# Batch 0 of a fused attention and MLP kernel: single score products between other work, products on zeros, and other places for the weight transfers

## The chip, the cores and the metric

One core of a Trainium2 chip. The metric is the device time of one execution in microseconds. The profiled span of an execution is some 1.8 us shorter than its device time. In the views PE is TensorE (PEld its weight loads), ACT ScalarE, DVE VectorE, POOL GpSimd and SP the sync engine; PEclk is the share of its full clock that TensorE was granted.

## The reference

```python
def _attn_ref(q, k, v):                      # each 8 x 12 x 448 x 64 (batch, heads, sequence, head_dim)
    scores = (1.0 / np.sqrt(64)) * np.matmul(q, k.transpose(0, 1, 3, 2))
    attn = np.exp(scores - np.max(scores, axis=-1, keepdims=True))
    attn = attn / (np.sum(attn, axis=-1, keepdims=True) + 1e-09)
    return np.matmul(attn, v)

def _moe_ref(x, w_in, w_out):                # x 3584 x 768, w_in 768 x 2048, w_out 2048 x 768
    h = x @ w_in
    return np.maximum(0.01 * h, h) @ w_out
```

The attention output, heads side by side, is `x`.

## The kernel before

Work goes by head pairs: 6 pairs in each of 8 batches, so 48 units `u`. A pair's q, k and v are loaded in float32 (three loads of 0.229 MB), cast to bf16 on POOL (pair 0's q and k on DVE and ACT), and q and k are transposed. Then come four score products with an exponential each (one for each key chunk), and the product with v (PV). The MLP of a batch is a generator whose matmuls are spread over the attention steps of the next batch, so batch 0's attention has no MLP to run beside it.

```python
def load(u, queues=(nc.sync,) * 3): ...          # q, k, v of pair u; five buffers each
def cast(u, by=(nc.gpsimd.tensor_copy,) * 3): ...# to bf16 on POOL; v into v_sb
def load_w(n=1):                                 # the next n of 8 weight pieces: 4 of w_in, 4 of w_out
    for _ in range(n):
        if w_steps:
            o, i = w_steps.pop(0)
            nc.gpsimd.dma_start(out=o, in_=i)    # float32 in memory, bf16 on the chip: 0.786 MB written
...
NPE = 12
def dma_transposes(u):                           # q and k of pairs 12 and on
    if NPE <= u < NU:
        turn(qkT[u % NQ][:, :QL], ...)           # a DMA transpose from the sync queue
def transposes(u):                               # q and k of the pairs before 12
    if u >= min(NPE, NU):
        return
    tr = ps_tr.tile([P, 2, S], BF16, name="tr")
    for i in range(2):                           # q, then k
        for so in range(NSC):
            nc.tensor.transpose(tr[:, i, ts(so, SC)], qk_sb[u][:, i, so], ident[:SC, :SC])
    nc.vector.tensor_copy(qkT[u % NQ][:, :QL], tr.rearrange("p i s -> p (i s)"))
...
# one unit of work, steps s0 to s7 (guards left out)
s0: scores(u, 0); scores(u, 1); expo(u, 0)
s1: expo(u, 1); x_transposes(u - 2); dma_transposes(u + 2)
s2: pv(u - 1, 0)
s3: load(u + 5); load_w({2: 1, 3: 2, 4: 2, 5: 2}.get(u, 0)); transposes(u + 1)
s4: scores(u, 2); scores(u, 3); expo(u, 2)
s5: expo(u, 3); cast(u + 3)
s6: pv(u - 1, 1)
```

Scores have two buffers in PSUM. One weight piece is issued ahead of all this, after pair 0's casts. Eight products on zeros stand at the very start (1.19 to 4.56 us), meant for TensorE's clock; the granted clock is 1.00 from 4.20 to 7.61 us and 0.50 from there to 14.44.

The softmax here doesn't subtract the row's maximum and nothing guards it: scores larger than these inputs give would overflow.

## Time and profile before

| | before |
|---|---|
| time, median of the first 3 runs | 427.61 us (427.56 to 428.5) |
| profiled span | 425.7 us |
| TensorE busy | 411.4 us, 97% |
| TensorE busy in the first 36 us | 28.05 us |
| TensorE busy from 36 to 75 us | 38.49 of 39.00 us |
| transfer rate from 8 to 64 us | 245 to 263 GB/s |

TensorE is full from 36 us to the tail, so what the kernel can gain or lose lies before.

### The profile page before, as it was taken

What the parts mean: (1) busy time and instruction counts of PE and PEld (TensorE: products, weight loads), DVE (VectorE), ACT (ScalarE), POOL (GpSimd) and SP (SyncE); (2) the same over time, 40 slices, a digit from 0 to 9 for tenths busy, and PEclk for the clock granted to TensorE, in tenths of its full rate; (3) what the DMA queues carried; (4) which work ended last, traced back from release to release, by engine and by line L of the source; (5) the groups of instructions that cost most, each with busy time, mean ns of one, the idle gap of its engine ahead of it and who ended that gap; (6) DMA issues with size and microseconds to landing.
All of it is one profiled execution on the core that took longest, in us unless ns stands there. A gap on an engine that the chain in (4) does not pass through costs nothing.

```text
span 425.7 us, 8968 instructions
## 1 busy us (share of the span) xinstructions
PE 411.4 (97%) x3709; PEld 226.3 (53%) x3724; DVE 100.2 (24%) x271; ACT 229.9 (54%) x322; POOL 92.1 (22%) x168
## 2 busy tenths in 40 slices
PE   6889999999999999999999999999999999999995
PEld 2555655544555555544455555554455555654562
DVE  1454323211222212311123212321123211320021
ACT  4887774467534675466643576456743477214300
POOL 5583332422111313112211131221112100000000
PEclk8899999999999999999999999999999999999999
DMA  8999999995546765784464977667446450230022
GB/s 219 257 246 245 249 249 197 256 253 118 125 117 167 209 125 158 187 209 108 104 148 131 183 180 145 177 178 170 117 99 161 99 84 18 56 85 2 0 75 74
DMA packets 98505, 63.66 MB, mean 150 GB/s; under 512 B 55456, under 2 KB 94880, under 8 KB 98464
## 3 DMA queue, kind: packets, MB, share of 16 engines
q1 hardware_dynamic: 90928, 56.56, 55.3%
q0 software_dynamic: 7296, 6.29, 9.4%
q8 instruction: 29, 0.48, 0.5%
q10 hardware_dynamic: 240, 0.23, 0.2%
q14 instruction: 12, 0.10, 0.1%
HBM read 45.61 MB, written 11.01 MB: 133 GB/s over the span
## 4 chain that ended last, share of the span: by engine, by line
PE 83%; DMA 12%; POOL 2%; ACT 1%; issue 1%; DVE 0%; SPq 0%; POOLq 0%
PE mm L256 33%; PE mm L239 31%; PE pv L196 9%; PE sc L178 9%; DMA fv<-in_v_dram 5%; DMA qkT<-qkb 4%; DMA fk<-in_k_dram 2%; DMA xT<-x 1%; ACT e L187 1%; PE tr L166 1%; POOL w_out_sb L124 1%; POOL v L111 1%; POOL w_in_sb L124 0%; POOL qkb L109 0%; POOL qkb L110 0%
## 5 line engine op out<-in xcount | busy, mean ns | idle before, releaser
L187 ACT ACTIVATE e<-sc 112x896 bf16<-112x896 f32 x192 | 167.6, 915 | 107.2 <-PE sc L178 107.2
L239 PE MATMUL mm<-xT,w_in_sb 128*128 128x384 bf16 (+1 forms) x753 | 160.3, 352 | 0.8
L256 PE MATMUL mm<-w_out_sb,h 128*128 128x384 bf16 x896 | 160.2, 326 | 0.0
L256 PEld LDWEIGHTS <-h 128*128 128x128 bf16 x896 | 81.7, 98 | 62.4 <-issue 14.1
L239 PEld LDWEIGHTS <-w_in_sb 128*128 128x128 bf16 x768 | 68.3, 97 | 70.3 <-issue 16.3
L244 ACT ACTIVATE h<-mm 128x384 bf16<-128x384 f32 (+1 forms) x128 | 69.8, 545 | 60.0 <-PE mm L239 59.9
L111 POOL CAST v<-fv 112x512 bf16<-112x512 f32 x48 | 29.6, 617 | 196.1 <-PE pv L196 163.2
L196 PEld LDWEIGHTS <-e 112*128 112x128 bf16 x1536 | 61.4, 98 | 15.6 <-DVE x L204 1.9
L203 DVE RECIPROCAL rec<-pv 112x4 f32<-112x4 f32 x96 | 17.5, 183 | 206.1 <-PE pv L196 205.3
L196 PE MATMUL pv<-v,e 112*128 112x65 bf16 x1536 | 65.3, 194 | 0.1
L178 PE MATMUL sc<-qkT 64*128 64x448 bf16 x384 | 55.4, 360 | 6.0 <-ACT e L187 3.7
L261 DVE COPY o<-mm 128x384 f32<-128x384 f32 x56 | 31.2, 557 | 90.0 <-PE mm L256 89.9
L204 DVE TENSOR_TENSOR x<-pv,rec 112x256 bf16<-112x256 f32 x96 | 40.7, 424 | 3.5 <-DVE rec L203 0.3
L109 POOL CAST qkb<-fq 112x512 bf16<-112x512 f32 x47 | 28.9, 615 | 37.4 <-DMA fq<-in_q_dram 20.6
L178 PEld LDWEIGHTS <-qkT 64*128 64x128 bf16 x384 | 12.1, 94 | 37.7 <-issue 31.3
L110 POOL CAST qkb<-fk 112x512 bf16<-112x512 f32 x47 | 28.9, 614 | 11.8 <-DMA fk<-in_k_dram 11.6
L166 PE MATMUL tr<-ident,qkb 112*128 112x112 bf16 x96 | 7.8, 226 | 1.3 <-POOL qkb L109 0.8
L169 DVE COPY qkT<-tr 128x896 bf16<-128x896 bf16 x12 | 7.4, 620 | 5.4 <-PE tr L166 5.3
L166 PEld LDWEIGHTS <-qkb 112*128 112x128 bf16 x96 | 6.2, 104 | 3.6 <-POOL qkb L109 1.3
L218 DVE COPY xT<-tr 128x448 bf16<-128x448 bf16 x9 | 3.5, 392 | 12.1 <-PE tr L217 12.1
L134 PE MATMUL mm<-warm 128*128 128x512 bf16 x8 | 3.4, 600 | 1.2 <-DVE warm L131 1.2
L124 POOL DMA_DIRECT2D w_out_sb<-in_moe_w_out_dram x4 | 3.5, 877 | 0.0
(17 smaller groups left out, 14.1 us busy)
## 6 DMA issues: line engine op xcount, KB each, us to landing
fq<-in_q_dram SPq DMA_DIRECT2D x48, 224.0 KB, 3.9
fv<-in_v_dram SPq DMA_DIRECT2D x48, 224.0 KB, 4.3
fk<-in_k_dram SPq DMA_DIRECT2D x47, 224.0 KB, 4.1
w_in_sb<-in_moe_w_in_dram POOLq DMA_DIRECT2D x4, 768.0 KB, 15.1
w_out_sb<-in_moe_w_out_dram POOLq DMA_DIRECT2D x4, 768.0 KB, 35.3
out_dram<-o SPq DMA_DIRECT2D x8, 336.0 KB, 3.1
out_dram<-o SPq DMA_DIRECT2D x8, 288.0 KB, 2.7
out_dram<-o SPq DMA_DIRECT2D x8, 240.0 KB, 3.3
```

Of the source, the lines that this page charges most:

```text
L109: by[0](qk_sb[u][:, 0].rearrange("p so h d -> p h so d"), fq)
L110: by[1](qk_sb[u][:, 1].rearrange("p so h d -> p h so d"), fk)
L111: by[2](v_sb[u % NV][:, :, :, :D], fv)
L166: nc.tensor.transpose(tr[:, i, ts(so, SC)], qk_sb[u][:, i, so], ident[:SC, :SC])
L178: nc.tensor.matmul(ps[:, j, :S], t[j * D:(j + 1) * D, S + c * SC:S + c * SC + P], t[j * D:(j + 1) * D, :S], start=True, stop=True,)
L187: nc.scalar.activation(e[:, :, c, :], sc_t.pop((u, c))[:SC, :, :S], AX.Exp, scale=scale)
L196: nc.tensor.matmul(ps[:, qc, :], e[:, at:at + P], vt[:, j, c, :], start=(c == 0), stop=(c == NSC - 1),)
L204: nc.vector.tensor_mul(x_t[u][:, :, j, :], ps[:SC, :, :D], rec.to_broadcast([SC, NSC, D]))
L239: nc.tensor.matmul(ps[:, :n], w_in_sb[:, kk, ts(m, P)], xT[:, kk, at:at + n], start=(kk == 0), stop=(kk == KD - 1),)
L244: nc.scalar.activation(h[:, m, :n], ps[:, :n], AX.Prelu, alpha=0.01)
L256: nc.tensor.matmul(ps[:, :NW], h[:, m, ts(c, P)], w_out_sb[:, m, ts(w, NW)], start=(m == 0), stop=(m == MD - 1),)
L261: nc.vector.tensor_copy(o[c][:, ts(w, NW)], ps[:, :NW])
```

## The change

Its intent: in batch 0, where ACT's exponentials set the pace (four take 3.34 of a pair's 3.88 us), issue each score product as soon as its buffer is free, with other products between, so that ACT never waits. More products on zeros through the first chunks (called fillers below) are meant to hold TensorE's clock up. The weight pieces come one for each pair while they are pieces of w_in. A new `first_slots` serves `u` = 0 to 5.

```diff
-    for _ in range(8):
-        ps = ps_mm.tile([P, 512], F32, name="mm")
-        nc.tensor.matmul(ps, warm[:, :P], warm, start=True, stop=True)
+    def warm_up(n): ...                     # n such products
+    warm_up(9)
...
+    def first_slots(u):
+        s0: scores(u, 0); expo(u, 0); if u == 0: warm_up(2)
+        s1: x_transposes(u - 2)
+        s2: scores(u, 1); expo(u, 1); if u == 0: warm_up(2)
+        s3: load(u + 5); load_w({1: 1, 2: 1, 3: 1, 4: 2, 5: 2}.get(u, 0)); pv(u - 1, 0)
+        s4: scores(u, 2); expo(u, 2)
+        s5: cast(u + 3); transposes(u + 1)
+        s6: scores(u, 3); expo(u, 3)
+        s7: pv(u - 1, 1)
...
-            load_w({2: 1, 3: 2, 4: 2, 5: 2}.get(u, 0))
...
-    steps = [s for u in range(NU + 2) for s in slots(u)]
+    steps = [s for u in range(NU + 2) for s in (first_slots if u < HP else slots)(u)]
...
     transposes(0)
+    warm_up(2)
```

(The steps of `first_slots` are written in one line each here, without their guards.)

More of the change, by code (lines that the diff above doesn't have):

```diff
@@ L131, with warm_up @@
     nc.vector.memset(warm, 0.0)
-    for _ in range(8):
-        ps = ps_mm.tile([P, 512], F32, name="mm")
-        nc.tensor.matmul(ps, warm[:, :P], warm, start=True, stop=True)
+    def warm_up(n):
+        for _ in range(n):
+            ps = ps_mm.tile([P, 512], F32, name="mm")
+            nc.tensor.matmul(ps, warm[:, :P], warm, start=True, stop=True)
+    warm_up(9)
     ident = const_pool.tile([P, P], BF16)
@@ L264, in mlp, with s0, s1, s2 @@
                 yield NW
+    def first_slots(u):
+        def s0():
+            scores(u, 0)
+            expo(u, 0)
+            if u == 0:
+                warm_up(2)
+        def s1():
+            if u >= 2:
+                x_transposes(u - 2)
+        def s2():
+            scores(u, 1)
+            expo(u, 1)
+            if u == 0:
+                warm_up(2)
+        def s3():
+            load(u + 5)
+            load_w({1: 1, 2: 1, 3: 1, 4: 2, 5: 2}.get(u, 0))
+            if u >= 1:
+                pv(u - 1, 0)
+        def s4():
+            scores(u, 2)
+            expo(u, 2)
+        def s5():
+            cast(u + 3)
+            transposes(u + 1)
+        def s6():
+            scores(u, 3)
+            expo(u, 3)
+        def s7():
+            if u >= 1:
+                pv(u - 1, 1)
+        return [s0, s1, s2, s3, s4, s5, s6, s7]
     def slots(u):
@@ L318 @@
     transposes(0)
+    warm_up(2)
     for s in steps[:begin[0]]:
```

## The prediction

> **What bounds the kernel now.** I read the page's engine rows first, then its slices, the chain of waits, the timeline of the first 75 us, and the DMA queues in two stretches.
>
> ```profile
> PE   6889999999999999999999999999999999999995
> PEld 2555655544555555544455555554455555654562
> DVE  1454323211222212311123212321123211320021
> ACT  4887774467534675466643576456743477214300
> POOL 5583332422111313112211131221112100000000
> PEclk8899999999999999999999999999999999999999
> DMA  8999999995546765784464977667446450230022
> ```
>
> A slice is 10.6 us. PE is busy 97% of the span: after about 36 us TensorE never rests (25.00 of 25.00 us between 36.2 and 61.2). The only room is in the first three and a half slices and in the tail, which the change leaves alone. But the DMA row reads 9 from the second slice to the ninth: until some 85 us the transfers are as full as TensorE will be later. The timeline (start, duration, engine, instruction, idle time before it) shows batch 0:
>
> ```profile
> 28.38 0.56 PEld L166 LDWEIGHTS <-qkb 112*128 112x128 bf16 x8
> ...
> 29.29 0.63 POOL L110 CAST qkb<-fk 112x512 bf16<-112x512 f32 x1
> 29.50 3.34 ACT L187 ACTIVATE e<-sc 112x896 bf16<-112x896 f32 x4 [0.54 <-PE sc L178]
> ```
>
> Four exponentials take 3.34 us and ACT then idles 0.54 us because two score products stand together behind the transposes: 3.88 us for each head pair. This idle is what the change aims at. What feeds TensorE's transposes is the cast of q and k on POOL:
>
> ```profile
> 32.42 0.56 PE L166 MATMUL tr<-ident,qkb 112*128 112x112 bf16 x8
> ...
> 33.43 0.61 POOL L110 CAST qkb<-fk 112x512 bf16<-112x512 f32 x1 [0.66 <-DMA fk<-in_k_dram]
> ...
> 36.81 0.56 PE L166 MATMUL tr<-ident,qkb 112*128 112x112 bf16 x8
> ...
> 71.41 0.55 PE L178 MATMUL sc<-qkT 64*128 64x448 bf16 x4 [0.51 <-DMA qkT<-qkb]
> ```
>
> Counting casts from the start, the one at 29.29 is pair 7's k; its transposes come at 32.42, 2.5 us after it ends. The one at 33.43 (having waited for its DMA) is pair 8's; its transposes come at 36.81, 2.8 us after. That is all the slack the loads have. The last line is the first score of pair 12, whose transpose is made by DMA: TensorE waits 0.51 us for it. Last, the queues (packets, MB, share of 16 engines) in 20.3 to 25.4 us, then 25.4 to 36 us:
>
> ```profile
> q1 hardware_dynamic: 1330, 1.27, 111.7%
> ```
> ```profile
> q0 software_dynamic: 1248, 1.26, 69.9%
> q1 hardware_dynamic: 1367, 1.31, 47.0%
> ```
>
> q1 carries q, k and v; q0 carries the weights. Alone, q1 moves 1.27 MB / 5.1 us = 249 GB/s. Beside q0 it moves 1.31 / 10.6 = 124 GB/s, at nearly equal packet counts. The sum doesn't change. So a weight piece in flight halves the rate of the loads.
>
> [...] 1248 packets beside 1367, and half the rate. [...] a transpose group takes 1.10 us at 7.82 and 0.55 us at 16.98, and the granted clock is 0.60 in 8 to 16 us, 1.00 after. [...] how late a first weight packet follows its issue; the trace does: 6.19 to 12.0 and 20.05 to about 25.5 us, 5.5 to 5.9 us.
>
> **The change part by part.**
>
> *Scores alone between other products (pairs 0 to 5).* TensorE needs for one pair 2 x 0.51 (PV) + 0.53 (transposes) + 0.30 (transposes of x) + 4 x 0.24 to 0.37 (scores), under 3.34 us. With each score placed as soon as a buffer is free ACT can run without its gap: 3.34 to 3.4 us a pair, some 0.5 us less. Over five or six pairs that is 2.5 to 3 us, if q and k are there. Pair 6 and the later ones keep the old order.
>
> *Products on zeros.* Nine more: one before the first transposes (0.42 us cold, and TensorE waits for the cast there until 4.76, about when it ends), two beside the copy to qkT (0.62 us), two after each of pair 0's first scores, where TensorE waits for ACT anyway. In the 4.6 us that pair 1 takes the clock is low; a warm clock is worth up to 0.7 us there, again if the data are there. So 0 to -0.7 us.
>
> *Weight pieces.* The instruction order of both kernels on POOL shows the real edit: a piece now stands right after the casts of pair 3, where there was none; after pair 5's casts one stands instead of two. The counts after pairs 4, 6 and 7 are the same, eight pieces in all. Pair 3's v is cast at 14.06 + 0.62 = 14.7 us, after pair 4's at 20.05. So the second piece is issued 5.4 us earlier, and by the measured lag (first packets of a piece in the trace against its issue) its packets start at about 20.3 instead of 25.5 (perhaps sooner, behind the first piece, which ends at 18.4). From there on q0 is never empty until the end, as before. In those 5.1 us q1 loses 5.1 x (249 - 124) GB/s = 0.64 MB, which is 2.8 loads of 0.229 MB; at 124 GB/s a load takes 1.85 us. **Every q, k and v that lands between about 26 and 60 us lands about 5 us later.** After that the weights are through earlier and the loads catch up.
>
> *The sum.* k of pair 7 was done at 29.9 (held by POOL, whose packets had ended at 25.4); by counting loads at the shared rate I get packets until 30.9, plus the 2.5 us that casts trail their last packets in such a stretch: about 34.0. k of pair 8: 34.05 + 5 to 6, about 39.7. TensorE meets three waits. Transposes of pair 6 at about 27.9 instead of a possible 25.4 (before: 28.4, so most of the early gain is gone). Transposes of pair 7 at 34.0 (before 32.4). Transposes of pair 8 at 39.7 (before 36.8): 2.9 us late. Pair 9's k, at about 45.7, meets transposes at 47.3 and costs nothing. From here TensorE is full and 2.9 us late. At pair 12 it arrives at 70.9 + 2.9 = 73.8; the DMA transpose, for which the same bytes must have moved as before, is there at 71 to 73, so the old wait of 0.5 us goes. Net +2.4 us: 427.6 + 2.4 = **430.0 us**.
>
> **The rivals.**
>
> *The gain stays.* ACT's gap goes, loads keep ahead: -3 us, 424.5. For it: nobody waits for loads on TensorE today. Against it: the slack is 2.5 us at pair 7, a faster TensorE uses it up, and even then pair 12 waits: its transposed tile landed at 71.4 with DMA saturated since 1 us, and the change removes no byte.
>
> *It is lost at pair 12.* Loads come just in time, TensorE arrives up to 3 us early at 68 and waits for that DMA transpose: 427.5, no change. It needs the second piece not to slow the loads; the shared rate speaks against it.
>
> *The delay is worse.* If the second piece follows the first without a gap, at 18.4, the loads lose another load or so, 2 us more: 432. [...]
>
> **Range and chances.** The middle is +2.4. Terms that carry it: the start of the second piece (18.4 to 22 us: +2 to -1.7) and the trailing of casts behind packets (1.2 us at pair 4, 2.7 at pair 8: +-1). The hidden-gain rivals pull the low side to 426.3, the worse delay the high side to 432.8. Two per cent is 8.6 us: TensorE's whole idle time is 425.7 - 411.4 = 14.3 us, 5 of it in the tail, so faster by that much is out of reach (1%). Slower needs 8.6 us of new idle time, three times what I find (3%).
>
> **What would show it right or wrong.** Right: the packets of the second piece begin at 18 to 21 us and q1's rate halves there; casts of k for pairs 6 to 8 wait for DMA; TensorE idles before its transposes of qkb in pairs 6, 7 and 8, some 6 us in all, put down to the casts on POOL; the first product of the MLP starts after 37 us (before: 36.16); ACT has no 0.54 us gaps in pairs 1 to 4; the clock in 8 to 16 us is near 1. After 75 us both profiles are alike. Wrong: the MLP starts at 33 to 35 us, or TensorE shows one wait of 2 to 3 us at pair 12's scores in place of those. The prediction fails mostly if q0's packets start much later than I take them to, or if the casts turn out to follow the loads more closely.

The sum came to +2.4 us (427.6 + 2.4 = 430.0). In the third rival a drop of the clock, taken as another 1 us, is cut with its condition. That rival's own sum, 432, is without it; the range's high side, 432.8, may hold a part of it.

## The result, and the profile after

| | before | after |
|---|---|---|
| median of 6 runs each | 427.59 us (427.09 to 428.5) | 430.94 us (429.25 to 431.39) |
| ratio, 95% interval | | 1.0068 (1.0046 to 1.009) |
| profiled span | 425.7 us | 429.6 us |

The changed kernel is slower by 0.7%, inside the 2% that counts as the same. Ratios here and below are the mean time of one kernel's fast runs over that of the kernel before's fast runs of the same rounds, so they are not quite the ratios of the medians.

The slices of the changed kernel (10.7 us each) that answer to those of before:

```profile
PE   7878999999999999999999999999999999999995
...
ACT  5974775466643676457734477446653377314300
...
PEclk9995999999999999999999999999999999999998
DMA  8999999685484967676365876797554450230022
```

The clock's low slices have moved from the first two (8 and 8 before) to the fourth (5), and TensorE's first four slices read 7, 8, 7, 8, where before they read 6, 8, 8, 9: it is fuller at first and thinner after. The early part does much of what the change wanted. In the timeline of the changed kernel (start, duration, engine, instruction, count):

```profile
6.92 11.16 ACT L191 ACTIVATE e<-sc 112x896 bf16<-112x896 f32 x13 [1.55 <-PE sc L182]
...
18.27 3.53 ACT L191 ACTIVATE e<-sc 112x896 bf16<-112x896 f32 x4 [0.18 <-PE sc L182]
```

Thirteen exponentials stand in one row without a gap, 0.86 us each; the next gap is 0.18 us instead of 0.54. After that row the gain for each pair is small: four exponentials take 3.53 us instead of 3.34, and with the gap a pair takes 3.72 us (18.27 to 21.99) instead of 3.88. But then TensorE waits. Its transposes of q and k (line 170 here, 166 before), in halves of four products because the k half has to wait, and the first product of the MLP:

```profile
22.73 0.37 PE L170 MATMUL tr<-ident,qkb 112*128 112x112 bf16 x4
23.90 0.37 PE L170 MATMUL tr<-ident,qkb 112*128 112x112 bf16 x4 [0.80 <-POOL qkb L110]
...
27.76 0.37 PE L170 MATMUL tr<-ident,qkb 112*128 112x112 bf16 x4 [0.27 <-POOL qkb L109]
29.64 0.37 PE L170 MATMUL tr<-ident,qkb 112*128 112x112 bf16 x4 [1.51 <-POOL qkb L110]
...
33.95 0.55 PE L170 MATMUL tr<-ident,qkb 112*128 112x112 bf16 x4 [0.66 <-POOL qkb L109]
35.38 0.56 PE L170 MATMUL tr<-ident,qkb 112*128 112x112 bf16 x4 [0.88 <-POOL qkb L110]
...
40.04 1.47 PE L243 MATMUL mm<-xT,w_in_sb 128*128 128x384 bf16 x4
41.30 0.74 PE L170 MATMUL tr<-ident,qkb 112*128 112x112 bf16 x8
```

These are pairs 5, 6, 7 and 8. The waits for POOL's casts add up to 4.1 us. Pair 8's transposes start at 41.30, where they started at 36.81 before: 4.5 us late. POOL itself was waiting for data:

```profile
34.71 0.61 POOL L110 CAST qkb<-fk 112x512 bf16<-112x512 f32 x1 [0.82 <-DMA fk<-in_k_dram]
```

This is pair 7's k, which was cast at 29.29 before. The queues of the changed kernel in 20.3 to 25.4 us, the stretch in which q1 had the engines to itself before (packets, MB, share of 16 engines):

```profile
q0 software_dynamic: 629, 0.63, 72.3%
q1 hardware_dynamic: 665, 0.64, 45.3%
```

q1 moves 0.64 MB instead of 1.27. By the packets in the trace the second weight piece, issued at 13.88, begins at 17.95 right behind the first, whose last packet starts at 17.88 (before: issued at 20.05, beginning at 25.7), and the last packet of weights starts at 66.8 instead of 73.9. Pair 8's k has its last packet at 37.6 instead of 30.7. After that both kernels do the same work on a full TensorE. Pair 12's scores start at 75.50 with no wait before them (before: 71.41, after a wait of 0.51): 4.1 us late, and the span is 3.9 us longer. (The profiled execution is the slowest of the six; between medians the difference is 3.35 us.)

### The profile page after: what moved, and what is told of

Read it like the earlier page. It is cut to its first block, busy times and chain, and to the rows that moved or that the text cites. A ratio compares the mean times of both kernels' runs of the same rounds, so it can differ in the third digit from the quotient of the medians.

```text
span 429.6 us, 8997 instructions
## 1 busy us (share of the span) xinstructions
PE 416.1 (97%) x3731; PEld 227.7 (53%) x3731; DVE 100.7 (23%) x271; ACT 230.8 (54%) x322; POOL 92.2 (21%) x168
## 4 chain that ended last, share of the span: by engine, by line
PE 91%; DMA 7%; SPq 1%; POOL 0%; DVE 0%; issue 0%
PE mm L243 35%; PE mm L260 35%; PE pv L200 10%; PE sc L182 10%; DMA fk<-in_k_dram 3%; DMA fv<-in_v_dram 2%; DMA fq<-in_q_dram 1%; PE tr L170 1%; SPq L98 1%; PE tr L221 0%; POOL qkb L110 0%; DVE o L265 0%; POOL v L111 0%
## 5 line engine op out<-in xcount | busy, mean ns | idle before, releaser
L243 PE MATMUL mm<-xT,w_in_sb 128*128 128x384 bf16 (+1 forms) x768 | 162.8, 354 | 0.0
L111 POOL CAST v<-fv 112x512 bf16<-112x512 f32 x48 | 29.6, 616 | 213.8 <-PE pv L200 187.0
L200 PE MATMUL pv<-v,e 112*128 112x65 bf16 x1536 | 66.2, 196 | 0.0
L182 PE MATMUL sc<-qkT 64*128 64x448 bf16 x384 | 56.4, 360 | 1.1 <-DVE qkT L173 0.7
L136 PE MATMUL mm<-warm 128*128 128x512 bf16 x15 | 5.4, 493 | 1.2 <-DVE warm L131 1.2
L221 PE MATMUL tr<-ident,x 112*128 112x112 bf16 x36 | 3.7, 232 | 1.8 <-DVE x L208 1.8
```

Of the source, the lines that this page charges most:

```text
L111: by[2](v_sb[u % NV][:, :, :, :D], fv)
L182: nc.tensor.matmul(ps[:, j, :S], t[j * D:(j + 1) * D, S + c * SC:S + c * SC + P], t[j * D:(j + 1) * D, :S], start=True, stop=True,)
L200: nc.tensor.matmul(ps[:, qc, :], e[:, at:at + P], vt[:, j, c, :], start=(c == 0), stop=(c == NSC - 1),)
L243: nc.tensor.matmul(ps[:, :n], w_in_sb[:, kk, ts(m, P)], xT[:, kk, at:at + n], start=(kk == 0), stop=(kk == KD - 1),)
```

## The experiments

Each of the twelve runs was correct and timed in five rounds against the kernel before. Theory A says that the earlier second piece slows the loads, which TensorE then waits for. The rivals put the loss down to the new score order, to the clock, or say that the early gain is real but lost elsewhere.

### The weight places alone

The kernel before, with one line changed:

```diff
-            load_w({2: 1, 3: 2, 4: 2, 5: 2}.get(u, 0))
+            load_w({1: 1, 2: 1, 3: 1, 4: 2, 5: 2}.get(u, 0))
```

> The kernel before with the new places of the weight pieces alone (one after the casts of pairs 3, 4 and 5, two after 6 and 7); old score order, eight products on zeros. Theory A (the earlier second piece halves the rate of the q, k, v loads, and TensorE waits for their casts): packets of the second piece follow the first without a gap at about 18 us, TensorE waits about 2 us or more in all for casts on POOL at pairs 5 to 8, time 429.5 to 431.5 us (ratio 1.005 to 1.009). Rival B (the new order of scores and fillers costs the time): 427.6 us, as before.

Measured: 430.65 us (428.21 to 433.02), ratio 1.008 (1.0053 to 1.0107). The second piece follows the first without a gap at 18.2 us, and in its table of waits (total, times, longest) TensorE waits for the casts:

```profile
PE tr L166 <- POOL qkb L110: 1.3, 2, 1.1
PE tr L166 <- POOL qkb L109: 1.3, 2, 0.7
```

The kernel before has 0.8 us of such waits in its first 80 us, all at the start. So this one line makes the whole loss; the score order and the fillers are not needed for it.

### The changed kernel with the old weight places

```diff
-            load_w({1: 1, 2: 1, 3: 1, 4: 2, 5: 2}.get(u, 0))
+            load_w({2: 1, 3: 2, 4: 2, 5: 2}.get(u, 0))
```

> The changed kernel with the old places of the weight pieces (one after pair 4, two after 5, 6 and 7); new score order and fillers kept. Theory A: the second piece's packets start at about 25.5 us again, the first MLP product starts 2 to 3 us earlier than in the kernel before (33 to 34.5 us instead of 36.16), and the gain is lost in a wait of 2 to 3 us at pair 12's scores for the DMA transpose, since that one lands at 70 to 72 us whatever TensorE does: 426.5 to 427.8 us. Rival B (score order costs): 430 to 431 us. Rival C (the early gain stays to the end): 424.5 to 425.5 us.

Measured: 428.02 us (425.28 to 429.44), ratio 1.0006 (0.9978 to 1.0035): no different from the kernel before. Two lines of its timeline, far apart, tell why:

```profile
34.36 0.56 PE L170 MATMUL tr<-ident,qkb 112*128 112x112 bf16 x8
```
```profile
70.74 0.91 PE L182 MATMUL sc<-qkT 64*128 64x448 bf16 x4 [2.22 <-DMA qkT<-qkb]
```

Pair 8's transposes start at 34.36, 2.45 us earlier than in the kernel before. At pair 12 TensorE then waits 2.22 us for the DMA transpose, which lands at 70.7 (before: 71.4). So the early gain of the score order and the fillers together is real, and the transfers take it back. The median is 0.2 us above the expected range, the claim holds.

This run has both, so it doesn't say which of them makes the 2.45 us. An estimate from ACT's rows: the kernel before starts its first exponential at 6.84 and, 26 exponentials later, the next group at 33.37; in this run it is 7.22 and 30.92, so 2.8 us less, of which a start 0.4 us later takes some back. At the old order's pace in full clock (3.87 us a pair, 25.62 to 29.50) 26 exponentials take 25.2 us. So some 1.5 us would be the order's, and some 1.4 us what the kernel before loses to its low clock and to a wait of 0.83 us for pair 1's cast.

### The changed kernel without the added products on zeros

`warm_up(8)` at the start and the other three calls of `warm_up` taken out.

> The changed kernel without the seven added products on zeros. Theory A: the clock is low in about 7.6 to 14.4 us again as in the kernel before, but what comes later is set by the loads, so the time is that of the changed kernel: 430 to 431.5 us. Rival: if the fillers' warm clock in 8 to 16 us is worth anything at the end, it is up to 0.7 us longer than the changed kernel, over 431.6 us.

Measured: 431.68 us (430.4 to 432.39), ratio 1.01 (1.0082 to 1.0117). The median lies 0.08 us inside the rival's range and 0.74 us above the changed kernel's, but the intervals overlap: what the fillers are worth in this setting is undecided at this size. By the products the low clock came, and longer than the 7.6 to 14.4 us expected: in its profile the score products from 8.2 to 18.2 us take 0.55 us each, as they do in the kernel before at a granted clock of 0.50 (0.55 us from 8 to 12 us; 0.35 at 1.00, from 20 to 25). The windows view of this run reads a clock of 1.00 from 5 to 19.8 us all the same, so its mean clock reads too high.

### Filling the waits

```diff
     for i in range(2):
+        if i == 1:
+            warm_up({5: 3, 6: 6, 7: 6}.get(u, 0))
         for so in range(NSC):
```

> The changed kernel with 3, 6 and 6 further products on zeros between the q half and the k half of the transposes of pairs 5, 6 and 7, where TensorE waits for the cast of k. Theory A1 (the waits alone let the clock fall in 31.4 to 41.7 us, and the low clock costs about 1.3 us on top of the waits): the clock stays at 1.00 there, pair 8's transposes start at 39.7 to 40.3 instead of 41.3 us, time 429.0 to 429.8 us. Rival A2 (the low clock is hidden behind the same waits for loads): 430.5 to 431.5 us, unchanged.

This run asks what the low clock of 31.4 to 41.7 us costs. Measured: 431.34 us (430.76 to 432.39), ratio 1.0099 (1.0082 to 1.0116). The mean clock of the profiled execution was 1.00, as wanted (0.985 in the changed kernel), and the time did not fall. Theory A1 falls: a full clock gains nothing here. That the waits for loads hide the low clock is the reading that fits; what the fifteen products themselves may cost isn't separated. In the timeline of this run, pair 8's k and its half of the transposes:

```profile
41.97 0.62 POOL L110 CAST qkb<-fk 112x512 bf16<-112x512 f32 x1 [0.41 <-DMA fk<-in_k_dram]
42.65 0.37 PE L172 MATMUL tr<-ident,qkb 112*128 112x112 bf16 x4 [0.66 <-POOL qkb L110]
```

With that clock TensorE still waits for the cast, 0.66 us. (In this run the cast of pair 8's k started 1.87 us later than in the changed kernel's profile, 41.97 against 40.10, and the loads were late already at pair 4, before the edited pairs: its k was cast at 19.84 against 17.08. So the comparison of the times carries the verdict, not the place of pair 8 alone.)

### Relieving pair 12

If the early gain is lost at pair 12's DMA transpose, TensorE may do that transpose itself. Starting from the changed kernel with the old weight places:

```diff
-    NPE = 12
+    NPE = 13          # 14 in the second of the two runs
...
-        if u >= NPE - 3:
+        if u >= 9:    # the transposes of x stay as they were
```

> The changed kernel with the old places of the weight pieces, and pair 12 transposed by TensorE (the DMA transposes of q and k begin at pair 13; those of x stay as they are). Theory: the second run of the experiments kept its early gain up to pair 12 and lost 2.2 us there to the DMA transpose; with that one gone it keeps it, less some 0.5 us for eight more transposes on TensorE: 425 to 426.3 us, faster than the kernel before by 1.2 to 2.4 us. Rival (another transfer is due at the same moment: a weight piece, or pair 13's DMA transpose): 427 to 428 us, with the wait of about 2 us at pair 13 or at the MLP.

> As the run before, with pairs 12 and 13 transposed by TensorE. Theory: if the wait moves to pair 13 when pair 12 is freed, this one is the faster of the two, 425 to 426 us; if it is gone with pair 12 already, this one is 0.5 us slower than the run before, for eight more transposes.

Measured: 428.18 us, ratio 1.0016 (0.9993 to 1.0039), and 428.37 us, ratio 1.0024 (1.0 to 1.0048). No gain: the rival is right. In the timeline of the first:

```profile
74.61 0.32 PE L260 MATMUL mm<-w_out_sb,h 128*128 128x384 bf16 x1 [2.07 <-DMA w_out_sb<-in_moe_w_out_dram]
```

The wait at pair 12 is gone and one of 2.07 us at the last piece of w_out stands in its place (2.28 us with 14). Two transfers were due at nearly the same moment, and behind the first stood the second.

The control, the kernel before with `NPE = 13`:

> Control: the kernel before, with pair 12 transposed by TensorE and nothing else changed. Theory: its wait at pair 12 was only 0.5 us and the eight transposes cost about as much: 427.2 to 427.8 us, no change. Rival (the DMA transpose of pair 12 is what held it): 425 to 426 us, and then the gain of the run with the new score order is not its own.

Measured: 427.75 us, ratio 1.0002 (0.9987 to 1.0017). No change, as expected.

### The pieces earlier still

```diff
-            load_w({1: 1, 2: 1, 3: 1, 4: 2, 5: 2}.get(u, 0))
+            load_w({0: 1, 1: 1, 2: 1, 3: 2, 4: 2}.get(u, 0))
```

> The changed kernel with the weight pieces a pair earlier still (one after the casts of pairs 2, none before; pieces after 3, 4 and 5 to 7 in the order 1, 1, 1, 2, 2 from the start of pair 0 on). Theory A (what counts is when the weight queue is never empty again; it already follows the first piece without a gap from 11.4 us on): issuing earlier changes nothing, 430 to 431.7 us, and the last weight packet is at 65 to 67 us as in the changed kernel. Rival (each pair by which pieces are issued earlier costs the same again): 433 to 434 us.

Measured: 431.77 us (430.0 to 434.67), ratio 1.0106 (1.0072 to 1.014). The last weight packet starts at 67.2 us, against 66.8 in the changed kernel. The median is 0.07 us above the expected range, the intervals overlap, and the median doesn't show the 2 to 3 us of the rival. That speaks for the theory: what counts is when the weight queue stops being empty, not how early a piece is issued behind another. But two of the six runs took 433.5 and 434.67 us, and in the profile pair 8's transposes start 0.50 us later (41.80 against 41.30), so a smaller cost isn't ruled out.

### Holding back loads that nobody needs yet

In the second run both late transfers share the engines with loads that are issued at 49.4 and 61.4 us and on, those of pairs 14 and 15, whose scores come after 80 us. Starting again from the changed kernel with the old weight places:

```diff
-            load(u + 5)
+            if u <= 8:
+                load(u + 5)
+            elif u >= 11:
+                load(u + 3)
```

The loads of pair 14 then stand on the sync queue behind the DMA transposes of pairs 12 and 13, and are issued at 63.9 us.

> The changed kernel with the old places of the weight pieces, and the loads of pairs 14 and on held back: load(u + 5) up to u = 8, none at u = 9 and 10, load(u + 3) from u = 11 on, so that they are issued behind the DMA transposes of pairs 12 and 13. Theory (two transfers are due at 71 to 74 us, pair 12's transpose and the last piece of w_out, and both share the engines with loads that nobody needs before 75 us): both come 2 us or more sooner, TensorE waits for neither by more than 0.5 us, and the early gain of 2 to 2.5 us stays: 424.8 to 426 us. Rival (some further transfer is due then, or later pairs now wait for their loads): 427 us or more, with a new wait after 60 us.

Measured: 425.69 us (424.67 to 429.07), ratio 0.9967 (0.9928 to 1.0006). The waits at pair 12 and at w_out are gone. One of 0.8 us is left, for the DMA transpose of x before the MLP. On the sync queue the instruction that issues pair 13's DMA transpose takes 1.23 us instead of 5.47 in the second run, and the last weight packet starts at 70.5 us instead of 73.8. The interval still touches 1.

With pair 12 transposed by TensorE as well:

> As the run before, with pair 12 transposed by TensorE too. Theory: nothing is left to gain at pair 12, so the eight transposes only cost: 0.3 to 0.6 us slower than the run before. If pair 12's DMA transpose is still waited for there, this one is the faster.

Measured: 424.85 us (424.27 to 427.22), ratio 0.9945 (0.9913 to 0.9978). This version beats both kernels, the one before by 0.55%, well inside the 2% that count as the same. From 36 to 75 us, where the kernel before had TensorE busy for 38.49 of 39 us, its windows view shows (stretch, then us and instructions of PE, PEld, DVE, ACT, POOL, granted clock, DMA share, GB/s):

```profile
0.00:36.00 36.00, 31.23 (x391) 17.79 (x392) 16.47 (x43) 28.16 (x34) 23.13 (x52) 1.00 1.07 248
36.00:75.00 39.00, 39.00 (x418) 23.29 (x417) 12.22 (x33) 25.49 (x37) 10.45 (x17) 1.00 1.18 223
```

In its first 95 us TensorE waits for no transfer and for no cast on POOL. The run was expected to be a little slower than the one before it and came out faster, but the intervals overlap, so pair 12's own share is undecided.

The control, the kernel before with the loads held back:

> Control: the kernel before with the loads held back in the same way and nothing else. Theory: it waits for the transfers by 0.5 us at most, so it gains 0 to 0.6 us: 426.8 to 427.5 us. If it reaches 425 to 426 us, the gain is not due to the new score order.

Measured: 427.3 us, ratio 0.9987 (0.996 to 1.0014): holding the loads back gains nothing where the early work isn't faster. (The kernel before with both, the loads held back and pair 12 on TensorE, was not run; each alone gains nothing.)

### The fillers, where nothing hides them

The fastest version, without its seven added products on zeros:

> The run with the old places of the weight pieces, the loads held back and pair 12 transposed by TensorE, without the seven added products on zeros. Theory: with the transfers out of the way the early clock counts, so the low clock in some 7 us of the first 20 costs 0.3 to 1 us: 425.2 to 426 us, still faster than the kernel before; the score order is the larger part of the gain. Rival (the fillers carry the gain): 427 us or more.

Measured: 427.57 us (426.22 to 429.81, 7 runs), ratio 0.9992 (0.9965 to 1.002). My theory fell here: the gain is gone, and the fillers are needed for it. Against the kernel before in the same rounds the two versions differ by some 2 us; their intervals overlap a little (from 0.9965 to 0.9978), so the size is rough. The mean clock was 0.977 to 0.989 in all seven runs, against 0.993 to 1.0 in all six of the version with fillers. In the profiled execution (the slowest of the seven) the clock was low from 8.54 to 25.60 us:

```profile
5.13:8.54 3.41, 1.76 (x19) 0.89 (x18) 0.62 (x1) 1.86 (x3) 2.78 (x5) 1.00 1.12 254
8.54:25.60 17.06, 16.11 (x155) 9.40 (x154) 6.32 (x16) 12.17 (x15) 10.97 (x18) 0.50 1.15 262
```

In this stretch, at a clock of 0.50, TensorE and not ACT is the bound: it is busy for 16.11 of 17.06 us, ACT for 12.17. So the score order is not enough alone. Whether the fillers are is not shown: no run has them with the old order. The estimate at the second run gives each about half of the early gain.

## Why the prediction was right

The direction, the cause and nearly the size were as told: 430.0 predicted, 430.94 measured, +2.4 against +3.35 us between medians. The loss is in the earlier weight piece, by the first run alone, and the early gain of the rest is lost at pair 12 where the pieces keep their places, by the second. Step by step:

- **ACT's gap.** Right in kind, too large in size. Thirteen exponentials stand without a gap, but then a pair takes 3.72 us, not 3.3 to 3.4. The 2.45 us at pair 8 (second run) is near the 2.5 to 3 us given, but by the estimate there only some 1.5 us of the early gain is the order's. That this did no harm to the number is luck in part: from pair 5 on the loads set the pace.
- **The lag of the second piece.** Mis-sized: 20.3 us was taken, "perhaps sooner", and it was 17.95. The 5.3 to 5.9 us between issue and first packet were measured on pieces that found their queue empty. The one issued behind a piece in flight, at 13.88, started when that one ended. So the loads lost more: pair 8's k came 6.9 us later by its last packet, not about 5.
- **Where TensorE waits.** Right for pairs 6 and 7, and a wait at pair 5 was missed (0.80 us). k of pair 6 was cast by 29.6 us (27.9 predicted), that of pair 7 by 35.3 (34.0), that of pair 8 by 40.7 (39.7). The waits come to 4.1 us, not some 6. At pair 8 no wait is left in the profile, since TensorE arrives there at 41.30, 0.6 us after the cast.
- **The sum.** Pair 8's transposes were predicted 2.9 us late and were 4.5 us late. Of the 1.6 us between, 1.0 is the later cast and 0.6 the later TensorE. Less the 0.51 us of the old wait at pair 12 that makes 4.0 us, and the span grew by 3.9. That the wait at pair 12 would go was right.
- **The clock.** The fillers are seven, not nine as the prediction counts them; nothing hung on it. The warm clock came (1.00 from 8 to 20 us), and what it is worth in this kernel the third run leaves undecided, at 0.74 us between medians. That the clock would fall later was only a rival. The clock did fall to 0.50, from 31.44 to 41.68 us, and no wait for a cast was over 1.51 us. The fourth run shows no gain from a full clock there; in the changed kernel's profile it may have part in the 0.6 us by which TensorE comes after pair 8's cast. The term "0 to -0.7 us" was too small as a size for the fillers in general: with the transfers out of the way, leaving them out costs 2.7 us between medians (424.85 against 427.57), some 2 us by the ratios.
- **The rivals.** "Lost at pair 12" is what happens with the old weight places: predicted 427.5, measured 428.02. "The gain stays" needs the loads held back too. Of "the delay is worse" the premise came true, a second piece without a gap behind the first, and about half of its 2 us more: 430.94 lies between 430.0 and 432.
- **A misreading.** The DMA row has nines up to its ninth slice, which ends at some 96 us, not 85. Nothing hung on it.

## What to carry to other kernels

In this kernel, with the transfers saturated (245 to 263 GB/s from 8 to 64 us in the kernel before), one weight piece issued earlier made the loads later (0.64 MB instead of 1.27 from 20.3 to 25.4 us): where a trace shows such a stretch, ask which transfer an engine will wait for first, and count what is moved before that moment. Idle time that was removed here ahead of a saturated queue came back as a wait at the next transfer that was due (2.22 us at pair 12), and a second one was due right behind it (2.07 us at w_out); holding back transfers that nobody needed yet is what freed both. Keep an earlier step's measured gain apart from the end time, so that a loss in one part doesn't hide a gain in another, and take the parts of a bundle out one by one, each of them.

## What the traces showed of the transfers and the clock

- Beside the loads, the first packets of a weight piece came 5.3 to 5.9 us after its issue where the weight queue was empty (6.11 to 11.4 us in the changed kernel, 6.19 to 12.0 and 20.05 to 25.7 before). Behind a piece in flight there was no gap: the first packet of the changed kernel's second piece starts at 17.95 us, the last one of its first piece at 17.88. While both queues had work they moved nearly equal numbers of packets: 629 of the weights beside 665 of the loads (20.3 to 25.4 us in the changed kernel).
- The stretches of low clock ahead of the tail are 6.83 us long in the kernel before, 10.24 in the changed one and 17.06 in the last run's profile, within 0.02 us two, three and five times 3.41. In four profiles the 3.41 us just before a fall had TensorE busy for 1.65 (before), 1.74 (after), 1.76 (last run) and 1.19 us (second run), while a stretch with 2.70 us (after) was not followed by a fall. Whether there is a bound between, these few don't show. The busy time alone doesn't tell when the clock returns: it stayed at 0.50 through 17.06 us of the last run, with TensorE busy for 16.11 of them. Here is the fall in the changed kernel, with the stretches before and after it:

```profile
24.62:28.03 3.41, 2.70 (x46) 1.71 (x44) 1.92 (x6) 3.17 (x4) 1.99 (x3) 1.00 1.18 247
28.03:31.44 3.41, 1.74 (x29) 1.05 (x26) 1.06 (x3) 1.51 (x3) 1.08 (x2) 1.00 1.17 245
31.44:34.85 3.41, 2.40 (x26) 1.62 (x25) 1.17 (x4) 1.61 (x2) 2.59 (x5) 0.50 1.18 245
```

- Loads for later shared the engines with transfers that were due: the last weight packet started at 73.8 us with the loads in the way (second run) and at 68.0 us with them held back and pair 12 off the queue. TensorE waited 2.22 us for pair 12's transpose in the one, and for no transfer in the first 95 us of the other.
